# Handing one phase of a two-phase kernel over to the next: where a scaling, two splits and a table load stand in ScalarE's and VectorE's order

## The chip, the cores and the metric

The kernel runs on one core of a Trainium2 chip. The metric is the device time of one execution in microseconds, median of several runs. Engines are named as in the profile: PE (TensorE, matrix products), PEld (its weight loads, which run beside the products), DVE (VectorE), ACT (ScalarE), POOL (GpSimd) and SP (SyncE, which issues nearly all DMAs). Each engine takes its instructions in the order in which the program lists them, and waits on semaphores for what other engines must have done.

## What is computed

An attention block without softmax, with a normed output, feeds a feed-forward block with the activation g = h * erf(softplus(h)). All of it is in float32.

```python
kv = np.einsum('bhsd,bhse->bhde', k, v)        # (8, 8, 576, 64) each
out = np.einsum('bhsd,bhde->bhse', q, kv)
rms = np.sqrt(np.mean(out * out, axis=-1, keepdims=True) + 1e-06)
x = (out / rms * g_norm)                       # then to (4608, 512)
h = x @ w_in                                   # (512, 2048)
sp = np.maximum(h, 0.0) + np.log1p(np.exp(-np.abs(h)))
g = h * erf(sp)
result = g @ w_out                             # (2048, 512)
```

## The kernel before

The 4608 tokens are worked off in nine tiles T of 512 tokens: 0 to 7 hold the first 512 tokens of each batch entry, tile 8 the 64 left over of all eight. The hidden width of 2048 is cut into 16 blocks of 128; one block of one tile is called a unit and is numbered n = 16 T + f. Four units make a batch.

A float32 product can be made of cheaper products in a reduced format (FP32R). For this each operand is *split* into three forms (lines 533 to 551): `upper` on ScalarE scales x by 1 + 2^-13 and stores it rounded ("high"); `lower` on VectorE makes "low" = x - high (L538) and "both" = 4096 low + high (L541). A product of split operands is then two sums in PSUM: n_ps, of the forms high and low (two products for each block of 128), and m_ps, of "both" (one product for each). The result is n_ps times 4095 plus m_ps, up to a scale that the weights carry: ScalarE scales n_ps into SBUF (`AF.Copy` with `scale=SHIFT - 1.0`), and VectorE's `add` (L575) adds m_ps.

There are two phases. In the first one, tiles 0 and 1, the weights stay in SBUF; the loop at `for n in range(FIRST * FC + 1)` goes through units 0 to 31, with the attention of the next tile in pieces between them (`steps`). Tile 0 uses plain float32 products, tile 1 mostly split ones. On the way the weights are split and written to DRAM. In the second phase, tiles 2 to 8, split weights are read back from DRAM for every batch, and each batch consists of four `hidden` products (h of four units) and four `result` products.

The hand-over between the phases is what the change concerns. It covers units 24 to 31. `whole` is 28, `BATCH` 4.

- Units 24 to 27 are *held*: their gated values (g = h * erf(softplus(h)), made by `gates` as one VectorE product of h and s, L904) aren't multiplied by the output weights within the loop. `hold` splits them into `g_held` while units 29 to 31 are worked on: unit 24 at n = 29, units 25 and 26 at n = 30, unit 27 at n = 31. `held_sums` then multiplies them by split weights that stayed in SBUF (`w_place`).
- For each unit n of tile 1 the loop issues: PE's `hidden` (n_ps, m_ps); the scaling of n_ps into h (ACT, L1030); the addition of m_ps (DVE, L575); gates of earlier units; splits of weights while there are any; Softplus (ACT, L1050); attention pieces; `hold`. From unit 28 on h goes to a tile `old_h`, which becomes the first batch of the second phase. The two banks with the tag `h` hold n_ps and m_ps of each unit in turn, so n_ps of a unit needs the scaling of the unit before to be done, and its m_ps the addition.
- `held_sums` runs when the loop is over. It lets the last attention piece of tile 2 do its `mean` (two products with mean_w, the table of log and exp, then Ln, Exp and Square on ScalarE, L476 to L478). On PE it issues the products of "both" of the held units into the four banks o_ps (which already hold the sums of units 16 to 23), and the n_ps sums of output groups j = 0 and 1, in the order units 24 and 25, unit 26, unit 27. Then `norm` (three VectorE steps, L484, L487, L496, and a transposition) gives x of the last quarter of tile 2, and `split` splits it into `x_forms`. A loop over j = 0 to 3 issues the n_ps sums of groups 2 and 3 (their banks are those of groups 0 and 1, so they wait for the scalings of these), the Erf of units 28 to 31 in twos, the scaling of n_ps[j] into e (L954), and the addition of o_ps[j] (L575).
- The gates of units 28 to 31 follow at the end of the loop. Then the pools of the first phase are closed, and pools of the second (w_out_p, for output weights) take their room; the first loads of output weights (`load_parts("out", BATCH)`, L845 on SP) wait until the last user of that room is done. w_in tiles of the first batch are loaded earlier, at n = 29 to 31.
- ScalarE's functions live in tables: one set for Ln and Exp (L113), one for Softplus (L116), one with Erf (loaded ahead of the first Erf that needs it, L960). Each change of set is a table load of its own.

The order of PE's, ScalarE's, VectorE's and SP's instructions is that of the program text (a manual schedule).

Of the kernel before, what the change touches and what calls it, by code (L numbers as in the profile page):

```python
# [50 lines left out]
BATCH = 4  # L51
# [18 lines left out]
def kernel(  # L70
# [462 lines left out]
    def upper(x, high):  # L533

        nc.scalar.activation(high, x, AF.Copy, scale=1.0 + 2.0**-13)  # L535
# [18 lines left out]
    def thirds(x, high, low, both):  # L554
        upper(x, high)
        lower(x, high, low, both)
# [346 lines left out]
    def gates(n):  # L903
        nc.vector.tensor_tensor(out=hs[n], in0=hs[n], in1=ss[n], op=ALU.mult)  # L904

    g_held = {}

    def hold(n):

        i = 2 * (n - whole + BATCH)  # L910
        tiles = [pair_tile("out", i + k, FP32R, "g_held") for k in range(2)]
        forms = g_held[n] = tiles[0][:, 0], tiles[0][:, 1], tiles[1][:, 0]
        thirds(hs[n], *forms)

    def held(ps, n, j, forms, start, stop):
        for form in forms:
            nc.tensor.matmul(  # L917
                ps,
                lhsT=g_held[n][form][:, j * P : j * P + P],
                rhs=w_held[n % FC][form],  # L920
                start=start and form == forms[0],
                stop=stop and form == forms[-1],
            )
# [5 lines left out]
    def held_sums():  # L929

        mean, norm, split = ending
        mean()
        units = range(whole - BATCH, whole)
        n_ps = [None] * J
        all_e = wide.tile([P, J, DM], FP32, name="e", tag="a")
        es.update((j, all_e[:, j]) for j in range(J))
        for j in range(2):
            n_ps[j] = ps_h.tile([P, G], FP32, name="n_ps", tag="h")
        for group in (units[:2], units[2:3], units[3:]):
            for n in group:  # L940
                both_held(n)
            for j in range(2):
                for n in group:
                    held(n_ps[j], n, j, (0, 1), n == units[0], n == units[-1])
        norm()
        split()
        for j in range(J):
            if j >= 2:
                n_ps[j] = ps_h.tile([P, G], FP32, name="n_ps", tag="h")
                for n in units:  # L950
                    held(n_ps[j], n, j, (0, 1), n == units[0], n == units[-1])
            if j >= 2:
                erf(range(whole + 2 * j - 4, whole + 2 * j - 2))
            nc.scalar.activation(es[j], n_ps[j], AF.Copy, scale=SHIFT - 1.0)  # L954
            add(es[j], o_ps[j])
        softplus_table()

    def erf(units):
        for i in units:
            nc.scalar.activation(ss[i], ss[i], AF.Erf)  # L960

    for n in range(FIRST * FC + 1):
        T, f = divmod(n, FC)
        if n == FC:
            early_room.close()
            late = ctx.enter_context(tc.tile_pool(name="late", bufs=1))
            x_new = ctx.enter_context(tc.tile_pool(name="x_new", bufs=1))
            acc = ctx.enter_context(tc.tile_pool(name="acc", bufs=1))
            w_in_p = ctx.enter_context(tc.tile_pool(name="w_in_p", bufs=BATCH))
            low = low_room.enter_context(tc.tile_pool(name="low", bufs=1))  # L970
            forms = late.tile([P, 3, KC, G], FP32R, name="x_forms0")
            x_forms[FIRST] = [forms[:, i] for i in range(3)]
        if T < FIRST:
            if f == 0:
                steps = pieces_of(T + 1)

            if due(0 if n == 2 * (BATCH - 1) else 1):
                weights()
            while kept:
                keep_prepared()  # L980
            for piece in steps[f][3]:
                piece()
            for key in list(w_new)[:2]:
                w_lower(*key)
            for piece in steps[f][0]:
                piece()
        while due(0):
            weights()
        done = n - LAG + 1
        if T == 0 and done >= 0:  # L990
            gates(done)
        if T == FIRST - 1:
            if f == 0:
                x_high = wide.tile([P, KC, G], FP32R, name="x_high", tag="a")
                x_low = low.tile([P, KC, G], FP32R, name="x_low")
                for i in range(0, KC, 2):
                    upper(xT[T][:, i : i + 2], x_high[:, i : i + 2])
                for i in range(0, KC, 2):
                    lower_only(xT[T][:, i : i + 2], x_high[:, i : i + 2], x_low[:, i : i + 2])
        if T == FIRST - 1 and f >= WHOLE:  # L1000
            n_ps, m_ps = hidden(T, f, turns=False)
        elif T < FIRST:

            if n >= AHEAD:
                plain[n] = ps_h.tile([P, G], FP32, name="h_ps", tag="h")
                blocks = [(n, c) for c in range(KC)]
            elif n == 0:
                for i, (pool, tag) in enumerate(((ps_now[0], "at"), (ps_now[0], "at"), (ps_o, "o0"))):
                    plain[i] = pool.tile([P, G], FP32, name="h_ps", tag=tag)
                blocks = [(i, c) for c in range(2) for i in range(2)]  # L1010
                blocks += [(2, 0), (2, 1)] + [(i, 2) for i in range(3)] + [(0, KC - 1)]
            else:
                blocks = [(n, KC - 1)]
            for i, c in blocks:
                nc.tensor.matmul(  # L1015
                    plain[i],
                    lhsT=blocks_of(one(w_in_sb, i % FC))[:, c],
                    rhs=xT[T][:, c, :],
                    start=(c == 0),
                    stop=(c == KC - 1),  # L1020
                )
        if T < FIRST:
            if n == whole:
                old_h = acc.tile([P, BATCH, G], FP32, name="h", tag="e")
            h = hs[n] = old_h[:, n - whole] if n >= whole else unit("h_sb")
            s = ss[n] = unit("s_sb")
            if n in plain:
                nc.scalar.copy(h, plain.pop(n))
            else:
                nc.scalar.activation(h, n_ps, AF.Copy, scale=SHIFT - 1.0)  # L1030
                add(h, m_ps)
            if T == FIRST - 1:
                if f == 1:
                    x_both = wide.tile([P, KC, G], FP32R, name="x_both", tag="b")
                    for i in range(0, KC, 2):
                        both_only(x_high[:, i : i + 2], x_low[:, i : i + 2], x_both[:, i : i + 2])
                    x_forms[T] = x_high, x_low, x_both
                if done < whole - 2:
                    gates(done)
                for key in list(w_new):  # L1040
                    w_lower(*key)
                for key in to_cut[f]:
                    w_upper(*key)
                if n == whole + 1:
                    gates(whole - 2)
                    gates(whole - 1)
            if T == FIRST - 1 and f and f % BATCH == 0:
                erf(range(n - BATCH // 2, n))
                softplus_table()
            nc.scalar.activation(s, h, AF.Softplus)  # L1050
            for piece in steps[f][1]:
                piece()
            for i in {whole + 1: (0,), whole + 2: (1, 2), whole + 3: (3,)}.get(n, ()):
                hold(whole - BATCH + i)
            if f % BATCH == BATCH - 1 and n < whole:
                apart = T == FIRST - 1 and f < FC - 1
                erf(range(n - BATCH + 1, n + 1 - (BATCH // 2 if apart else 0)))
                if not apart:
                    softplus_table()
            if T == FIRST - 1:  # L1060
                load_parts("in", {FC - 3: 2, FC - 2: 1, FC - 1: 1}.get(f, 0))
        if LAG <= n < whole - BATCH + LAG:
            T2, f2 = divmod(n - LAG, FC)
            last = n - LAG == FC - 1
            project(f2, hs[n - LAG], last)
            if last:
                sums(acc, "e")
                for j in range(J):
                    store(T2, j, es.pop(j))
        if n == FIRST * FC:  # L1070
            held_sums()
        if T < FIRST:
            for piece in steps[f][2]:
                piece()
            fetch_some(4)
    for n in range(whole, FIRST * FC):
        gates(n)


# [187 lines left out]
```

## Time and profile before

| what | us |
|---|---|
| median of 3 runs | 910.99 (910.78 to 911.67) |
| the profiled execution, whole | 910.55 |
| its span (first to last instruction) | 908.8 |
| products of the second phase, from the first hidden product to the end | from 241.34 |
| PE busy, DVE busy, ACT busy in the span | 897.4, 765.1, 594.7 |

The span is what the trace covers; the execution around it takes 1.75 us more. A row of the timeline gives start, length, engine, line, operation, output and input tiles, number of instructions, and in brackets how long the engine had been idle before it and what it waited for. Consecutive instructions of a kind overlap a little in the records: products of 128x512 start 0.228 us apart and last 0.39 us each; ACT functions of 128x512 start 0.52 us apart and last 0.58 to 0.63; DVE steps of that size start 0.60 us apart, or 0.72 if one needs the one before, and last 0.69.

### The profile page before, as it was taken

To read this page: it belongs to the slowest core of one execution; us is meant where nothing else is said; L and a number is where in the kernel's file an instruction comes from. 1 tells how busy PE (TensorE), PEld (TensorE's weight loads), DVE (VectorE), ACT (ScalarE), POOL (GpSimd) and SP (SyncE) were. 2 spreads that over 40 slices of the span, in tenths; PEclk is the share of its full clock that TensorE was granted. 3 is DMA by queue.
4 is the path that set the end of the run, shared out by engine and by line. 5 is a ranking of instruction groups with operands and counts; after the bars stand their busy time and mean duration, and the time that the engine had idled before them with its cause. 6 is when DMAs were issued, how large, how long until landed. Compare 5 with 4: busy or idle time off the path is not lost.

```text
span 908.8 us, 13463 instructions
## 1 busy us (share of the span) xinstructions
PE 897.4 (99%) x4954; PEld 673.0 (74%) x4954; DVE 765.1 (84%) x1103; ACT 594.7 (65%) x789; POOL 4.7 (1%) x14
## 2 busy tenths in 40 slices
PE   8999999999899999999999999999999999999998
PEld 4444446666688888888888888888888888888886
DVE  5899959998688888888888888888898888887777
ACT  5976667776766667666666666666666766665552
POOL 2000000000000000000000000000000000000000
PEclk9999999999999999999999999999999999999999
DMA  9967308999399988999899879988797778778871
GB/s 283 296 221 232 101 24 292 363 348 359 121 383 376 354 298 268 368 316 316 274 326 370 302 254 318 366 300 304 282 351 261 270 302 311 290 286 314 324 265 50
DMA packets 137505, 259.89 MB, mean 286 GB/s; under 512 B 78880, under 2 KB 87328, under 8 KB 137440
## 3 DMA queue, kind: packets, MB, share of 16 engines
q1 hardware_dynamic: 136704, 258.09, 80.7%
q10 hardware_dynamic: 544, 0.82, 0.3%
q8 instruction: 39, 0.64, 0.3%
q14 instruction: 26, 0.21, 0.1%
q0 software_dynamic: 192, 0.13, 0.1%
HBM read 224.40 MB, written 34.60 MB: 285 GB/s over the span
## 4 chain that ended last, share of the span: by engine, by line
PE 92%; DVE 3%; DMA 2%; ACT 2%; SPq 0%; issue 0%; DVEq 0%
PE n_ps L600 48%; PE m_ps L600 24%; PE o_ps L656 9%; PE h_ps L1015 6%; PE at_ps L426 2%; PE at_ps L412 2%; DMA w_out_parts<-w_out 1%; DMA q_sb<-in_q_dram 1%; PE at_ps L465 1%; PE at_ps L464 1%; PE n_ps L917 1%; DMA w_raw<-in_moe_w_out_dram 1%; DVE w_in_sb L282 0%; DVE h L904 0%; DVE w_e L277 0%
## 5 line engine op out<-in xcount | busy, mean ns | idle before, releaser
L600 PE MATMUL n_ps<-w_out_parts,g_forms 128*128 128x512 f32 (+1 forms) x936 | 231.1, 389 | 0.1
L600 PE MATMUL n_ps<-x_forms,w_in_parts 128*128 128x512 f32 x896 | 224.0, 392 | 0.0
L600 PEld LDWEIGHTS n_ps<-w_out_parts,g_forms 128*128 128x128 f32 x936 | 173.8, 188 | 35.6 <-DMA w_out_parts<-w_out 0.6
L600 PEld LDWEIGHTS n_ps<-x_forms,w_in_parts 128*128 128x128 f32 x896 | 166.8, 188 | 35.1
L575 DVE TENSOR_TENSOR h<-m_ps,h 128x512 f32<-128x512 f32 x116 | 78.1, 687 | 59.3 <-PE m_ps L600 57.2
L600 PE MATMUL m_ps<-w_out_parts,g_forms 128*128 128x512 f32 x464 | 124.1, 390 | 0.0
L600 PE MATMUL m_ps<-x_forms,w_in_parts 128*128 128x512 f32 x448 | 119.8, 390 | 0.0
L1173 ACT ACTIVATE h<-n_ps 128x512 f32<-128x512 f32 x112 | 66.1, 593 | 74.6 <-PE n_ps L600 74.4
L1178 ACT ACTIVATE s<-h 128x512 f32<-128x512 f32 x112 | 68.4, 629 | 70.7 <-DVE h L575 70.6
L600 PEld LDWEIGHTS m_ps<-w_out_parts,g_forms 128*128 128x128 f32 x464 | 87.2, 188 | 18.5
L600 PEld LDWEIGHTS m_ps<-x_forms,w_in_parts 128*128 128x128 f32 x448 | 84.2, 188 | 17.4
L575 DVE TENSOR_TENSOR e<-m_ps,e 128x512 f32<-128x512 f32 x116 | 80.1, 692 | 15.2 <-PE m_ps L600 5.3
L656 PE MATMUL o_ps<-w_out_sb,h_sb 128*128 128x512 f32 x192 | 87.0, 596 | 0.0
L541 DVE SCALAR_TENSOR_TENSOR g_forms<-g_forms 128x1024 fp32r<-128x1024 f32 x58 | 71.1, 1225 | 2.0
L538 DVE TENSOR_TENSOR g_forms<-h,g_forms 128x1024 fp32r<-128x1024 f32 x58 | 70.6, 1217 | 1.2 <-ACT g_forms L535 1.1
L535 ACT ACTIVATE g_forms<-h 128x1024 fp32r<-128x1024 f32 x58 | 58.4, 1049 | 16.9 <-PE m_ps L600 11.1
L570 DVE SCALAR_TENSOR_TENSOR e<-n_ps,e 128x512 f32<-128x512 f32 (+1 forms) x89 | 60.4, 678 | 7.3 <-PE n_ps L600 7.3
L1015 PE MATMUL h_ps<-xT,w_in_sb 128*128 128x512 f32 x144 | 65.1, 596 | 1.2 <-DVE w_in_sb L282 1.1
L1227 DVE TENSOR_TENSOR h<-h,s 128x1024 f32<-128x1024 f32 x56 | 65.9, 1217 | 0.0
L656 PEld LDWEIGHTS o_ps<-w_out_sb,h_sb 128*128 128x128 f32 x192 | 35.6, 190 | 38.2 <-issue 37.3
L116 ACT ACT_TABLE_LOAD x43 | 55.2, 1283 | 0.8
L1015 PEld LDWEIGHTS h_ps<-xT,w_in_sb 128*128 128x128 f32 x144 | 27.0, 190 | 35.3 <-issue 31.3
(147 smaller groups left out, 1033.9 us busy)
## 6 DMA issues: line engine op xcount, KB each, us to landing
w_out_parts<-w_out SPq DMA_DIRECT2D x116, 768.0 KB, 6.9
w_in_parts<-w_in SPq DMA_DIRECT2D x112, 768.0 KB, 6.7
w_in<-w_new SPq DMA_DIRECT2D x16, 768.0 KB, 4.5
k_sb<-in_k_dram SPq DMA_DIRECT2D x32, 288.0 KB, 5.7
v_sb<-in_v_dram SPq DMA_DIRECT2D x31, 288.0 KB, 5.9
w_raw<-in_moe_w_in_dram SPq DMA_DIRECT2D x16, 512.0 KB, 5.8
w_raw<-in_moe_w_out_dram SPq DMA_DIRECT2D x8, 1024.0 KB, 5.3
out_dram<-e SPq DMA_DIRECT2D x32, 256.0 KB, 3.6
```

The source lines that it names most:

```text
L116: nc.scalar.preload_act_table_set("softplus")
L535: nc.scalar.activation(high, x, AF.Copy, scale=1.0 + 2.0**-13)
L538: nc.vector.tensor_tensor(out=low, in0=x, in1=high.bitcast(FP32), op=ALU.subtract)
L541: nc.vector.scalar_tensor_tensor(out=both, in0=low.bitcast(FP32), scalar=SHIFT, in1=high.bitcast(FP32), op0=ALU.mult, op1=ALU.add,)
L570: nc.vector.scalar_tensor_tensor(out=out_, in0=ps, scalar=scale, in1=out_, op0=ALU.mult, op1=ALU.add)
L575: nc.vector.tensor_tensor(out=out_, in0=ps, in1=out_, op=ALU.add)
L600: nc.tensor.matmul(ps[:, cols], lhsT=weights(form, k), rhs=moving(form, k)[:, cols], start=(form == forms[0] and k == 0), stop=(form == fo ...
L656: nc.tensor.matmul(o_ps[j], lhsT=g[:, j * P : j * P + P], rhs=one(w_out_sb, f), start=(f == 0), stop=last,)
L1015: nc.tensor.matmul(plain[i], lhsT=blocks_of(one(w_in_sb, i % FC))[:, c], rhs=xT[T][:, c, :], start=(c == 0), stop=(c == KC - 1),)
L1173: nc.scalar.activation(h[:, i], n_ps, AF.Copy, scale=SHIFT - 1.0)
L1178: nc.scalar.activation(s[:, i], h[:, i], AF.Softplus)
L1227: nc.vector.tensor_tensor(out=part(h, half), in0=part(h, half), in1=part(s, half), op=ALU.mult)
```

## The change

It reorders what ScalarE and VectorE do from unit 29 to the end of `held_sums`.

- `hold` is parted into `hold_upper` (ScalarE) and `hold_lower` (VectorE). The upper parts of units 24 and 25 come at n = 29, of 26 and 27 at n = 30; the lower parts of 24 and 25 at n = 30, of 26 and 27 at n = 31, each behind the addition to h of that n.
- Three gates in one place (units 25, 26 and 27 at n = 29) become two (25, 26) there and one (27) at n = 30, behind the addition to h.
- In `held_sums`, the set with Erf is named right behind `norm`; the scaling of group 0 is issued ahead of `split`, that of group 1 behind it. The n_ps sums of groups 2 and 3, additions of groups 0 and 1, Erf and gates of units 28 and 29, scaling of group 2, Erf of 30, scaling of group 3, Erf of 31, and the additions of groups 2 and 3 follow in that order. The gates of units 30 and 31 remain behind `held_sums`.

```diff
-    def hold(n):
+    def hold_upper(n):
...
-        forms = g_held[n] = tiles[0][:, 0], tiles[0][:, 1], tiles[1][:, 0]
-        thirds(hs[n], *forms)
+        g_held[n] = tiles[0][:, 0], tiles[0][:, 1], tiles[1][:, 0]
+        upper(hs[n], g_held[n][0])
+
+    def hold_lower(n):
+        lower(hs[n], *g_held[n])
...
         norm()
+
+        def scaled(j):
+            nc.scalar.activation(es[j], n_ps[j], AF.Copy, scale=SHIFT - 1.0)
+
+        nc.scalar.preload_act_table_set("sigmoid_and_others")
+        scaled(0)
         split()
-        for j in range(J):
-            if j >= 2:
-                n_ps[j] = ps_h.tile([P, G], FP32, name="n_ps", tag="h")
-                for n in units:
-                    held(n_ps[j], n, j, (0, 1), n == units[0], n == units[-1])
-            if j >= 2:
-                erf(range(whole + 2 * j - 4, whole + 2 * j - 2))
-            nc.scalar.activation(es[j], n_ps[j], AF.Copy, scale=SHIFT - 1.0)
+        scaled(1)
+        for j in range(2, J):
+            n_ps[j] = ps_h.tile([P, G], FP32, name="n_ps", tag="h")
+            for n in units:
+                held(n_ps[j], n, j, (0, 1), n == units[0], n == units[-1])
+        for j in range(2):
+            add(es[j], o_ps[j])
+        erf((whole, whole + 1))
+        for n in (whole, whole + 1):
+            gates(n)
+        scaled(2)
+        erf((whole + 2,))
+        scaled(3)
+        erf((whole + 3,))
+        for j in range(2, J):
             add(es[j], o_ps[j])
         softplus_table()
...
-                if done < whole - 2:
-                    gates(done)
+                if n <= whole + 2:
+                    gates(done + max(0, n - whole - 1))
...
                 if n == whole + 1:
                     gates(whole - 2)
-                    gates(whole - 1)
...
-            for i in {whole + 1: (0,), whole + 2: (1, 2), whole + 3: (3,)}.get(n, ()):
-                hold(whole - BATCH + i)
+            for i in range(*{whole + 1: (0, 2), whole + 2: (2, 4)}.get(n, (0,))):
+                hold_upper(whole - BATCH + i)
+            for i in range(*{whole + 2: (0, 2), whole + 3: (2, 4)}.get(n, (0,))):
+                hold_lower(whole - BATCH + i)
...
-    for n in range(whole, FIRST * FC):
+    for n in range(whole + 2, FIRST * FC):
         gates(n)
```

## The prediction

> **What bounds the kernel now.** I read the page's busy table first, then the chain of waits. TensorE is busy for 99% of the span, so a gain can only come from the little that is left.
>
> ```profile
> span 908.8 us, 13463 instructions
> PE 897.4 (99%) x4954; PEld 673.0 (74%) x4954; DVE 765.1 (84%) x1103; ACT 594.7 (65%) x789; POOL 4.7 (1%) x14
> ```
>
> A table of stretches gives PE 642.87 us busy out of 643 us from 262 us to 905 us. Nothing waits there, so whatever the middle of the kernel gains or loses reaches the end unchanged. The middle is 217 to 256 us, where the first phase hands over to the second. The chain of waits, asked for 205 to 262 us, leaves PE at 217.1 us and comes back only for one stretch:
>
> ```profile
> 223.05 0.69 DVE h L575
> ...
> 228.97 0.52 ACT g_held L535
> 229.49 0.02 issue
> 229.50 1.28 ACT L113
> ...
> 232.19 0.64 ACT u L478
> ...
> 234.30 0.76 DVE x L496
> ...
> 235.09 0.63 ACT x_forms L535
> 235.72 0.49 ACT e L954
> 236.21 0.04 issue
> 236.25 5.26 PE n_ps L917 x16
> ```
>
> Columns: start, length, what. Softplus of the last unit and the split of unit 27 hold ScalarE until 229.5 us. Then come the root's table, three functions, three VectorE steps of the norm, the split's scaling of x (L535), and only then the scaling of the first sums (L954), which empties the bank that PE waits for. PE's timeline shows both halts:
>
> ```profile
> 223.79 1.20 PE L600 MATMUL m_ps<-x_both,w_new 128*128 128x512 f32 x4 [0.63 <-DVE h L575]
> 236.25 5.25 PE L917 MATMUL n_ps<-w_place,g_held 128*128 128x512 f32 x16 [3.04 <-ACT e L954]
> ```
>
> The brackets hold idle time and releaser. The second row also takes 5.25 us for 16 products. The table of stretches says why (PE, PEld, DVE, ACT, POOL busy, then PEclk):
>
> ```profile
> 235.00:237.00 2.00, 0.74 (x2) 0.65 (x3) 1.93 (x4) 1.89 (x4) 0.00 (x0) 0.67 0.00 0
> 237.00:239.00 2.00, 2.00 (x7) 1.52 (x6) 1.37 (x3) 1.99 (x3) 0.00 (x0) 0.50 0.00 0
> 239.00:241.00 2.00, 2.00 (x10) 1.66 (x9) 0.67 (x1) 1.45 (x4) 0.00 (x0) 0.97 0.00 0
> ```
>
> The granted clock is half until about 239 us. Last, the waits of the weight loads and of SP's queue between 195 and 262 us:
>
> ```profile
> PEld n_ps L600 <- DMA w_out_parts<-w_out: 0.6, 1, 0.6
> SPq L845 <- DVE h L904: 15.9, 1, 15.9
> ```
>
> The second phase's first output weights are requested only after the last gate product (L904, ending at 245.26 us). They land at 255.39 us and hold PE once more.
>
> **What the skill says.** TensorE: Matmul & The Clock Gate, section "Part 1: The HAM clock gate", has PE fall to half its clock after an idle window of some 3.4 us and return after as long busy. This trace roughly agrees: 3.04 us idle, then half clock for some 3 us; after 0.63 us idle the clock stayed 1.00. The same page, "Architectural detail", calls ScalarE and VectorE strict FIFO; here the scaling at 235.62 us stood behind L535 though its sums were complete at about 232.8 us. ScalarE: Activation LUTs, "What ACT_TABLE_LOAD costs", gives 1283 ns plus 1380 ns of drain. The load itself is 1.28 us here too, but the next function starts 0.02 us later, so I take 1.28. The same page, "Table sets", lists erf in the sigmoid set and cheap functions in every set, so the copies under the early table need no other load; that copies need none is seen here (scalings run under the log table at 235.62 us).
>
> **The change part by part.** The built programs show PE's and SP's orders unchanged, and no instruction added or dropped. ScalarE and VectorE are reordered from 217 us on. I carry the old starts forward: VectorE starts 0.60 us apart (0.72 when dependent), ScalarE 0.52, PE 0.228 per product.
>
> *Splits in twos.* After gates of units 25 and 26 (217.80, 218.40), the four steps of unit 24's split and the third gate no longer stand ahead of the attention step. That step waits for its square (219.03) and runs 219.05 to 221.2. The addition to h of unit 30 then waits only for its product (221.32): 221.41 to 222.10, formerly 223.05. So m_ps of unit 31 starts right behind its n_ps at 222.99, not 223.79: 0.80 saved. Late next: gate 27 at 222.01, then splits of 24 and 25, the last ending at 225.35 (formerly 226.37). PE wants it at 225.30, so the old stall of 0.47 at L917 shrinks to about 0.1, and PE is now 1.02 ahead. h of unit 31 is added at 225.26 to 225.95; the 0.24 stall of the second bank goes, making about 1.2. Splits 26 and 27 end at 227.27 and 228.60, ahead of their products (228.2 and 230.0). PE ends its first sums at about 232.0, formerly 233.2.
>
> On ScalarE, g_held 26 and 27 (ready 223.7) and the copy of h (223.68 to 224.28) precede softplus of unit 31 at 225.97. With no g_held behind it, the root's table starts at 226.61, formerly 229.50: 2.89 earlier. The three functions end at 229.94 and x is normed at 234.30 - 2.89 + 0.76 = 232.17.
>
> *Erf's table sooner.* The load runs 229.95 to 231.23, while PE is on its first sums and VectorE on the norm: cost nothing. It used to stand at 236.71, behind the scalings.
>
> *Scaling ahead of the split.* The first sum's last two products started at 232.14 before and were complete at about 232.14 + 2 x 0.228 + 0.16 (a product's record lasts 0.39) = 232.76; now 232.76 - 1.2 = 231.56. Its scaling runs 231.60 to 232.20 with nothing in front, and PE starts its third sum at 232.24, formerly 236.25: 4.01 saved (1.2 of it is the part above). PE's gap is some 0.3 us, so I expect no half clock: 16 products take 16 x 0.228 = 3.65 instead of 241.34 - 236.25 = 5.09, saving 1.44. The split of x goes at 232.2, the second scaling at 232.72 to 233.3, in time for the fourth sum at 234.06; the remaining steps of the split end at 234.3. PE enters the second phase at about 235.9, formerly 241.34. **Together 5.45 us.**
>
> *Additions, Erf and gates interleaved.* VectorE: additions at 234.2 and 234.8, gates 28 and 29 at 235.4 and 236.0, additions at 236.6 and 237.2 (third and fourth scalings end at 234.9 and 236.7), gates 30 and 31 at 237.8 and 238.4, ending at 239.09. Formerly 245.26: 6.17 earlier. The last Erf ends at 237.2, so the last gate waits for none. SP's request moves by as much, with the DMA queues just as empty (0.00 busy before it in both). Landing at 255.39 - 6.17 = 249.22 meets PE wanting the fourth tile at 254.87 - 5.45 = 249.42. The stall of 0.56 goes: **5.45 + 0.56 = 6.0 us.** What queues behind the request on SP (k, v, w_in) moves with it. The fourth w_in tile, requested at 228.02 for a use now at 245.6, has 17 us; the longest landing there is 10.8. Each hidden product's banks come free ahead of use (the tightest: fourth scaling ending at 236.7, bank wanted at 237.7).
>
> *What is unknown.* Whether the half clock really goes: between 0 and 1.44 saved; I take 1.44 since 0.63 idle cost nothing. Whether the weights land in time: between a stall of 0.56 + 0.8 (if they land a microsecond slower) and none; I take none, as they meet an empty queue in both. The added waits on ScalarE: at worst the norm is late and holds the second scaling behind x's split; its slack is 0.76, and another microsecond would cost 0.3. On the other side PE's remaining gaps (0.3 + 0.1) bound any further gain at 0.4.
>
> The profiled execution took 910.55 us around its span of 908.8; its span becomes 902.8 and the execution 904.55. It stands 0.44 below the median of 910.99, which gives 910.99 - 6.0 = **905.0**.
>
> **The rivals.**
> - *Half clock stays* (8%): the short gap falls into an unlucky window. For: the window's phase isn't seen. Against: 0.63 us idle at 1.00. 4.01 + 0.56 stay: 911.0 - 4.6 = 906.4.
> - *Additions not freed* (6%): unit 30's addition is still late, through the square or the attention step. PE keeps its 0.63 halt and ScalarE's chain slips alike: 0.8 less, 905.8.
> - *Weights are the real bound* (3%): the output weights land near the old 255.4, because something besides the gate holds their request, and PE merely waits longer there. For: they did hold PE. Against: SP's 15.9 us wait ends at the gate. 911.0, no change.
> - *Slower* (5%): the new phase between PE and DMA makes the 0.56 stall on w_out recur at each of the 28 batches' first output products. DMA is busy for 0.67 to 1.05 of its time after 262 us. At 0.56 each it costs 15.7 against 6.0 gained: 920.7. It decides from 6.0 / 28 = 0.21 us per batch. Against: the gate moves 6.17 and PE 6.0, so the phase hardly changes, and it never recurred before.
> - The forecast itself: 78%.
>
> **How the numbers follow.** About 0.2% (1.8 us) is what a measurement of this kernel can tell from no change. Forecast and the first two rivals lie beyond that: faster 0.92. The third gives same 0.03, the fourth slower 0.05. The forecast's own 0.4 below, its unknowns of up to about 1.4 above, the first two rivals and the medians' scatter (0.9 in three runs) make 903.8 to 907.4.
>
> **What would show it.** PE's m_ps of unit 31 without the L575 wait; the third and fourth of the held units' n_ps sums starting near 232.2 after under 0.5 us idle, 3.7 us long at clock 1.00; the first second-phase product near 236; the last gate ending near 239; no weight-load wait on w_out_parts. I am wrong if PE still idles over 1 us between 231 and 236, if the clock dips, or if any PE wait appears after 250 us.

## The result and the profile after

| | before | after |
|---|---|---|
| median, 6 runs each | 911.19 (909.11 to 911.67) | 904.27 (904.04 to 904.75) |
| the profiled execution, whole / span | 910.55 / 908.8 | 904.33 / 902.5 |

The ratio is 0.9927, with a 95% interval of 0.9915 to 0.9940: 5.5 to 7.7 us faster. The forecast was 905.0.

The first two lines of the page show how little PE's total says: its busy time falls by 2.5 us only, while the span falls by 6.3. The rest of the gain is idle time that is gone.

```profile
span 902.5 us, 13462 instructions
PE 894.9 (99%) x4954; PEld 671.3 (74%) x4954; DVE 765.2 (85%) x1103; ACT 594.7 (66%) x789; POOL 4.7 (1%) x14
```

The chain of waits for 205 to 262 us, which before left PE for 19 us at 217.1, stays on PE now and leaves it once, for two thirds of a microsecond (start, length, what):

```profile
230.68 0.47 PE n_ps L920 x2
231.15 0.02 issue
231.17 0.61 ACT e L951
231.78 0.04 issue
231.82 3.94 PE n_ps L920 x16
235.76 1.84 PE n_ps L600 x8
```

L951 is the scaling that was L954, L920 the held units' products that were L917. The scaling starts 0.02 us after the first sum is complete. PE's timeline (start, length, line, tiles, idle before and its releaser) has the gap, the 16 products, the first hidden product and the first result product:

```profile
231.82 3.94 PE L920 MATMUL n_ps<-w_place,g_held 128*128 128x512 f32 x16 [0.24 <-ACT e L951]
235.59 2.01 PE L600 MATMUL n_ps<-x_forms,w_in_parts 128*128 128x512 f32 x8
...
248.03 1.98 PE L600 MATMUL n_ps<-w_out_parts,g_forms 128*128 128x512 f32 x8
```

The eight products of that last row took 0.42 us longer before, with a wait for the output weights inside:

```profile
253.78 2.40 PE L600 MATMUL n_ps<-w_out_parts,g_forms 128*128 128x512 f32 x8
```

The table of stretches (PE, PEld, DVE, ACT, POOL busy, PEclk, DMA share, GB/s) has full clock in every stretch from 230 to 900 us; before, it stood at 0.50 for one such stretch and at 0.67 for the one ahead of it:

```profile
231.00:233.00 2.00, 1.76 (x8) 1.17 (x7) 1.97 (x3) 1.83 (x4) 0.00 (x0) 1.00 0.46 126
233.00:235.00 2.00, 2.00 (x11) 1.62 (x10) 1.97 (x5) 1.93 (x4) 0.00 (x0) 1.00 0.00 0
```

ScalarE's timeline shows the new order: root's table, Erf's table, first scaling, x's split, second scaling.

```profile
226.17 1.28 ACT L113 ACT_TABLE_LOAD   x1
...
229.50 1.28 ACT L953 ACT_TABLE_LOAD   x1
231.17 0.60 ACT L951 ACTIVATE e<-n_ps 128x512 f32<-128x512 f32 x1 [0.39 <-PE n_ps L920]
231.75 0.63 ACT L535 ACTIVATE x_forms<-x 128x512 fp32r<-128x512 f32 x1
232.29 0.58 ACT L951 ACTIVATE e<-n_ps 128x512 f32<-128x512 f32 x1
```

And SP waits 9.8 us for the last gate where it waited 15.9. The output weights are requested at 238.69 us; before, it was 245.41 (SP's timeline, of before first, then of after):

```profile
SPq L845 <- DVE h L904: 9.8, 1, 9.8
```

```profile
245.41 2.03 SPq L845 DMA_DIRECT2D w_out_parts<-w_out  x4
```

```profile
238.69 2.16 SPq L845 DMA_DIRECT2D w_out_parts<-w_out  x4
```

Two traces don't start alike: PE reaches the attention product ahead of unit 30 (L412), the last mark in front of everything the change touches, at 217.01 us before and at 216.52 after. That 0.49 us belongs to the start of the kernel. To keep it out, the traces are compared from that product on, at two places: B, the first hidden product of the second phase, and C, the first product of the second result group. From C to the end of the span every trace takes 651.3 or 651.4 us, so what a kernel gains up to C it keeps.

| run | median us | L412 | B - L412 | C - L412 | C against before |
|---|---|---|---|---|---|
| before | 911.19 | 217.01 | 24.33 | 40.41 | |
| after | 904.27 | 216.52 | 19.07 | 34.70 | -5.71 |
| e1 pairs only | 906.72 | 216.89 | 20.17 | 36.79 | -3.62 |
| e2 sums only | 906.76 | 216.54 | 21.52 | 37.16 | -3.25 |
| e3 table late | 904.87 | 217.02 | 19.34 | 35.07 | -5.34 |
| e4 split first | 905.80 | 216.62 | 20.15 | 35.78 | -4.63 |
| e5 gap filled | 909.11 | 215.78 | 23.03 | 39.63 | -0.78 |
| e6 gap part filled | 910.41 | 216.55 | 24.61 | 40.77 | +0.36 |
| e7 gates last | 905.10 | 216.97 | 19.08 | 35.22 | -5.19 |
| e8 after again | 904.47 | 216.70 | 19.09 | 34.71 | -5.70 |
| e9 sum first | 904.26 | 216.43 | 18.70 | 34.37 | -6.04 |
| e10 gates first | 904.36 | 216.86 | 18.69 | 34.39 | -6.02 |

e6 has one time, the others are medians. The median of the kernel before differed between the batches of runs: 910.55 beside e1 to e4, 910.62 beside e5 to e7, 909.97 beside e8 to e10. Part of the reason is in the last of the experiments.

### The profile page after: what moved, and what is told of

It reads as the page before. It is cut to its first block, busy times and chain, and to the rows that moved or that the text cites. A ratio compares the mean times of both kernels' runs of the same rounds, so it can differ in the third digit from the quotient of the medians.

```text
span 902.5 us, 13462 instructions
## 1 busy us (share of the span) xinstructions
PE 894.9 (99%) x4954; PEld 671.3 (74%) x4954; DVE 765.2 (85%) x1103; ACT 594.7 (66%) x789; POOL 4.7 (1%) x14
## 4 chain that ended last, share of the span: by engine, by line
PE 97%; DVE 1%; ACT 1%; DMA 1%; issue 0%; DVEq 0%; SPq 0%
PE n_ps L600 49%; PE m_ps L600 24%; PE o_ps L656 9%; PE h_ps L1031 6%; PE at_ps L426 2%; PE at_ps L412 2%; PE n_ps L920 1%; PE at_ps L464 1%; PE at_ps L465 1%; PE warm_ps L803 1%; DMA w_raw<-in_moe_w_out_dram 1%; PE o_ps L920 0%; DVE w_e L277 0%; PE o_ps L723 0%; DVE w_in_sb L282 0%; PE ms_ps L730 0%
```

## The experiments

### The two halves of the change alone: e1 and e2

e1 keeps the reordered splits and gates and takes `held_sums` as it was. e2 does the reverse.

```diff
 # e1, against the changed kernel; the gates also go back behind everything
-        nc.scalar.preload_act_table_set("sigmoid_and_others")
-        scaled(0)
         split()
-        scaled(1)
...
+        for j in range(J):
...
+                erf(range(whole + 2 * j - 4, whole + 2 * j - 2))
+            nc.scalar.activation(es[j], n_ps[j], AF.Copy, scale=SHIFT - 1.0)
+            add(es[j], o_ps[j])
```

> The change with only its first part: splits in twos and the third gate behind the addition to h; the sums of the held units as in the kernel before. My theory: the two PE halts of 0.63 and 0.24 go and ScalarE reaches the root's table 2.9 us sooner, so the first sums' scaling ends about 3.3 us sooner even behind x's split; PE's gap shrinks from 3.04 to about 1.3, no half clock, PE enters the second phase some 4.6 us sooner, and the output weights (gates all at the end) hold it again for about 0.8: 906.2 us, 5.0 below the kernel before. Rival (this part is worth only the two halts, and the gain sits in the scaling moved ahead): 910.0 us, PE gap near 3, clock still dips.

> The change with only its second part: Erf's table sooner, the scaling ahead of x's split, Erf, gates and additions interleaved; splits as in the kernel before. My theory: the root's chain is as late as before, so the first scaling ends at about 234.75 and PE starts again 1.45 us sooner than before after a gap of 1.6; no half clock, another 1.4; the weights' stall of 0.56 goes: 907.8 us, 3.4 below before. If the clock still dips, 909.2. Rival (the parts add up to the whole, so with 5.0 of 6.9 in the pairs only 1.9 are left here): 909.3 us with a clock of 1.00.

e1: 906.72 us, ratio 0.9955 (0.9939 to 0.9972). e2: 906.76 us, ratio 0.9957 (0.9942 to 0.9972). PE's timelines, of e1 first, then of e2 (the scaling L951 has another line number in each kernel: L957 in e1, L948 in e2):

```profile
233.28 3.94 PE L920 MATMUL n_ps<-w_place,g_held 128*128 128x512 f32 x16 [1.32 <-ACT e L957]
...
251.73 0.73 PE L600 MATMUL n_ps<-w_out_parts,g_forms 128*128 128x512 f32 x2 [0.72 <-DMA w_out_parts<-w_out]
```

```profile
234.31 3.92 PE L917 MATMUL n_ps<-w_place,g_held 128*128 128x512 f32 x16 [1.57 <-ACT e L948]
```

Gaps of 1.32 and 1.57 us stand where 1.3 and 1.6 were expected, the products take 3.9 us in both, so the clock stays full in both. In e1 the late gates turn part of the gain into a wait for the output weights, as expected, but the whole is less than I expected: 3.62 us at C and 3.8 in the medians of its batch, for 5.0. PE enters the second phase 4.16 us sooner (B, 24.33 - 20.17) where I had put 4.6, and the weights take back 0.54. My 5.0 didn't follow from its own parts, which allow for about 4.4 (4.6 less the 0.24 by which the stall was to grow from 0.56 to 0.8). The rival of e1, which left only the two small halts to the pairs, is out. The additive rival of e2 asked for a rest of 1.9; 3.25 came. The halves overlap: 3.62 + 3.25 = 6.87 against 5.71 for both. Each alone leaves the clock full, and the 1.3 us of the half clock can be won only once; that it is the main part of the overlap is argued, not tried by itself.

In e2 ScalarE's timeline shows what becomes late next if the chain to the root isn't sooner: the table load itself.

```profile
232.36 1.28 ACT L950 ACT_TABLE_LOAD   x1
233.66 0.60 ACT L948 ACTIVATE e<-n_ps 128x512 f32<-128x512 f32 x1
```

The scaling follows the load after 0.02 us, and the first sum had been complete for more than a microsecond (its last two products started at 231.67). Only with the pairs does the early load lie in PE's shadow.

### The early table and the early scaling, each taken out: e3 and e4

```diff
 # e3
-        nc.scalar.preload_act_table_set("sigmoid_and_others")
 # e4
-        scaled(0)
         split()
+        scaled(0)
```

> The changed kernel without the early naming of Erf's table, which then stands ahead of the first Erf, behind the second scaling. My theory: it delays the third scaling from 233.97 to about 235.2, which still frees its bank within 0.3 us of PE wanting it, and the last gate by 0.2 us: 904.5 us, within 0.3 of the changed kernel's 904.3. Rival (the load on the path costs its whole length): 905.6 us, 1.28 above, all of it a PE wait before the first hidden product.

> The changed kernel with x's split ahead of the first scaling again, all else as changed. My theory: the scaling starts at about 232.3 instead of 231.17, PE's gap grows from 0.24 to about 1.3, the clock stays 1.00, and the weights' request slips by less than PE: 905.4 us, 1.1 above the changed kernel's 904.3. Rival (this order is the main part, some 4 us, half clock included): 908 us or more, clock dipping to 0.50.

e3: 904.87 us, ratio 0.9937 (0.9922 to 0.9952). At C it is 0.37 later than the changed kernel, a little more than the 0.3 I allowed and far from the rival's 1.28. The load now stands behind the second scaling, and the third, which frees the bank of the first hidden product, comes late (ScalarE's timeline, then the waits of the weight loads):

```profile
233.38 1.28 ACT L975 ACT_TABLE_LOAD   x1
234.67 1.15 ACT L975 ACTIVATE s_sb<-s_sb 128x512 f32<-128x512 f32 x2
235.73 0.58 ACT L951 ACTIVATE e<-n_ps 128x512 f32<-128x512 f32 x1
```

```profile
PEld n_ps L600 <- ACT e L951: 0.5, 1, 0.5
```

e4: 905.80 us, ratio 0.9947 (0.9932 to 0.9962), at C 1.08 later than the changed kernel; 1.1 was expected. PE's gap is 1.31, the clock full:

```profile
233.01 3.92 PE L920 MATMUL n_ps<-w_place,g_held 128*128 128x512 f32 x16 [1.31 <-ACT e L951]
```

So within the whole change, by one trace each, the early scaling is worth 1.1 us and the early table 0.4.

### The half clock by itself: e5 and e6

```diff
 # e5: range(3); e6: range(1), the kernel before otherwise
-            held(o_ps[j], n, j, (2,), False, n == whole - 1)
+            held(o_ps[j], n, j, (2,), False, stop)
...
+        for again in range(3):
+            both_held(whole - 1, again == 2)
         norm()
         split()
```

> The kernel before with PE's idle stretch filled: the four products of 'both' of unit 27 are issued three times more behind the first sums (the output then has that term four times), nothing else moves. My theory: the gap shrinks from 3.04 to about 0.3, the clock stays 1.00 and the 16 products take 3.9 instead of 5.25, so PE enters the second phase 1.3 sooner; but the output weights are requested as late as before, so their stall grows from 0.45 to about 1.8 and the time stays at that of the kernel before, within 0.3 us. Rival (the half clock is a loss of its own, on the path): 1.3 below before. Second rival (the half clock isn't due to idling): 5.25 us for the 16 products again.

> The kernel before with the same four products issued once more (that term is in the output twice), which leaves a gap of about 2.1 us. Gaps of 1.3 and 1.6 us left the clock at 1.00 in the runs so far, one of 3.04 halved it. My theory: 2.1 is still short enough, clock 1.00, 16 products in 3.9. Rival: any gap over 2 halves it, about 5.2.

e5, 909.11 us, ratio 0.9988 (0.9981 to 0.9995). PE's timeline:

```profile
231.83 2.88 PE L917 MATMUL o_ps<-w_place,g_held 128*128 128x512 f32 x12
235.03 3.94 PE L917 MATMUL n_ps<-w_place,g_held 128*128 128x512 f32 x16 [0.32 <-ACT e L956]
...
253.44 0.73 PE L600 MATMUL n_ps<-w_out_parts,g_forms 128*128 128x512 f32 x2 [0.68 <-DMA w_out_parts<-w_out]
```

Twelve products that change nothing in the order of any other engine give the clock back: the 16 products take 3.94 instead of 5.25, and B is 1.30 sooner. The times say the same: each of the 20 runs of e5 lists a mean granted clock of 0.999 or 1.000, while 15 of the 23 runs of the kernel before in that batch list 0.995 to 0.998. So the idle stretch brings the half clock about; it doesn't do so in every execution, as the other eight of the 23 show (below, two groups of times). My theory erred about the rest. I had the weights' request fixed; it went out at 243.21 - 215.78 = 27.43 us behind L412, in the kernel before at 245.41 - 217.01 = 28.40, because the third and fourth scaling, and with them Erf, the additions and the gates, wait for those 16 products. So 0.78 of the 1.30 arrive at C, and the weights take the other 0.52. The ratio of the times gives 1.1 us, with an interval of 0.5 to 1.7. So neither my theory (no change, within 0.3 us) nor the first rival (1.3 us) came out; the truth lies between.

e6 leaves a gap of 2.17 us, and the clock dips all the same, but later (table of stretches):

```profile
235.00:237.00 2.00, 1.20 (x5) 1.02 (x6) 1.97 (x4) 1.98 (x4) 0.00 (x0) 1.00 0.00 0
237.00:239.00 2.00, 2.00 (x7) 1.53 (x7) 0.91 (x2) 1.99 (x4) 0.00 (x0) 0.57 0.00 0
239.00:241.00 2.00, 2.00 (x7) 1.57 (x6) 0.69 (x1) 1.21 (x3) 0.00 (x0) 0.57 0.00 0
```

PE started again at 235.80 and ran at full clock for more than a microsecond before it was halved; the 16 products took 5.53. My theory, that 2.1 us is short enough, is wrong. e6 has one run; in e1, e2 and e4, with gaps of 1.31 to 1.57 us, all 12 runs list 0.999 or 1.000. So 2.17 us can be enough, and with 1.57 us or less it was never seen.

### The weights' request: e7

```diff
-        for n in (whole, whole + 1):
-            gates(n)
...
-    for n in range(whole + 2, FIRST * FC):
+    for n in range(whole, FIRST * FC):
         gates(n)
```

> The changed kernel with the gates of units 28 and 29 back behind all additions, with those of 30 and 31; Erf and scalings as changed. My theory: VectorE then waits for the fourth scaling with work left, the last gate ends about 0.9 later (239.5 instead of 238.6 on the changed kernel's clock), PE's entry into the second phase doesn't move, and as the fourth tile of output weights landed only 0.1 to 0.2 before PE wanted it, PE waits about 0.7 for it: 905.0 us against 904.3. Rival (the request had slack): 904.3 and no wait on the output weights.

905.10 us, ratio 0.9938 (0.9922 to 0.9955). VectorE's timeline shows the empty place that the two gates had filled, PE's the wait:

```profile
236.88 0.69 DVE L575 TENSOR_TENSOR e<-o_ps,e 128x512 f32<-128x512 f32 x1 [0.81 <-ACT e L951]
237.49 2.49 DVE L904 TENSOR_TENSOR h<-h,s_sb 128x512 f32<-128x512 f32 x4
```

```profile
250.25 0.73 PE L600 MATMUL n_ps<-w_out_parts,g_forms 128*128 128x512 f32 x2 [0.24 <-DMA w_out_parts<-w_out]
```

The request is 240.04 - 216.97 = 23.07 us behind L412, in the changed kernel 22.17: 0.90 later. B doesn't move, C is 0.52 later. So the weights had about 0.4 us to spare in the changed kernel (0.90 - 0.52, if the transfers took as long in both), where I had put 0.1 to 0.2, and gates between the additions are worth half a microsecond.

### Further along the same path: e8, e9, e10

e9 moves the gate of unit 27 behind the splits of 24 and 25, and the n_ps products of unit 27 ahead of its products of "both". e10 puts the last gates ahead of the last additions as well. e8 is the changed kernel beside them.

```diff
 # e9 and e10
-        for group in (units[:2], units[2:3], units[3:]):
+        for group in (units[:2], units[2:3]):
...
+        for j in range(2):
+            held(n_ps[j], units[-1], j, (0, 1), False, True)
+        both_held(units[-1])
...
-                if n <= whole + 2:
-                    gates(done + max(0, n - whole - 1))
+                if n <= whole + 1:
+                    gates(done)
...
+            if n == whole + 3:
+                hold_upper(whole - 1)
...
+            if n == whole + 2:
+                gates(whole - 1)
 # e10
-        erf((whole + 2,))
+        erf((whole + 2, whole + 3))
         scaled(3)
-        erf((whole + 3,))
+        for n in (whole + 2, whole + 3):
+            gates(n)
```

> The changed kernel as it is, beside the two that follow: 904.3 us, 0.9927 of the kernel before, within 0.4 us.

> The changed kernel with the third gate (unit 27) behind the splits of units 24 and 25, unit 27's scaled form behind the copy of h, and the n_ps products of unit 27 ahead of its products of 'both'. My theory: the stall of 0.37 on the split of unit 25 and PE's gap of 0.24 in front of the third sum both go nearly, so PE enters the second phase 0.4 sooner; the weights' request hangs on VectorE's unbroken row of steps behind x and doesn't move, but had some 0.4 to spare: 903.9 us, with a wait on the output weights just about to appear. Rival (the table load of Erf's set now ends last, so nothing is gained): 904.3 us.

> As the one before, and with the last Erf ahead of the fourth scaling and the gates of units 30 and 31 ahead of the third and fourth additions. My theory: the last gate ends 1.2 sooner, the request goes out as much sooner, PE's entry is as in the one before, so no wait on output weights even with the gain: 903.9 us, or 0.1 less than the one before if that one met a wait. Rival (late scaling or additions hold the banks of the first hidden products): slower than the changed kernel, with a PE wait between 235 and 243.

e8: 904.47 us, ratio 0.9937 (0.9924 to 0.9950); its trace repeats the first one's to 0.02 us. e9: 904.26 us, ratio 0.9937 (0.9924 to 0.9950). e10: 904.36 us, ratio 0.9940 (0.9926 to 0.9953). The times of the three can't be told apart. The 903.9 that I expected of e9 and e10 was not reached. The trace of e9 shows what was wanted: hardly any idle time in front of the 16 products (0.09 us from the end of the record ahead, in the changed kernel 0.23), B 0.37 and C 0.33 sooner than there. The scaling now stands straight behind the table load, which ends last, as the rival had it.

```profile
231.35 3.94 PE L920 MATMUL n_ps<-w_place,g_held 128*128 128x512 f32 x16
```

```profile
229.41 1.28 ACT L956 ACT_TABLE_LOAD   x1
230.70 0.60 ACT L954 ACTIVATE e<-n_ps 128x512 f32<-128x512 f32 x1
```

In e10 the request goes out 1.19 us sooner (237.84 - 216.86 = 20.98 against 22.17), and yet a short wait appears:

```profile
PEld n_ps L600 <- DMA w_out_parts<-w_out: 0.2, 1, 0.2
```

In its table of stretches the queues moved 215 GB/s in the microsecond from 241 us and 276 in the next; in the changed kernel's they ran at 399 and 430 in these two. So an earlier request isn't by itself an earlier landing. Why the transfers were slower there wasn't tried. The rival of e10 is out: B is as in e9 (18.69 and 18.70).

### Two groups of times before: e11 and e12

> The kernel before as it is, one more look. Its times over the runs so far fall in two groups, 908.4 to 909.5 and 910.3 to 911.9, with little between; those of the changed kernel and of the one with PE's gap filled don't. My theory: the two groups are executions in which the clock dips in PE's gap of 3.04 us or doesn't, so a profiled execution near 908.9 has 16 products in about 3.9 at a clock of 1.00, and one near 911 has them in about 5.2 with the clock at 0.50. Rival (the groups come from the start of the kernel, whose length varies by 1.2 us between traces): the 16 products take about 5.2 in either group.

> The same once more, as one look may fall in the same group as the first trace: near 908.9 us with the 16 products in about 3.9 at a clock of 1.00, or near 911 with about 5.2; the rival has about 5.2 in both groups.

Both executions fell into the upper group (910.74 and 910.78 us) and repeat the first trace: 5.42 and 5.37 us for the 16 products.

```profile
236.26 5.42 PE L917 MATMUL n_ps<-w_place,g_held 128*128 128x512 f32 x16 [3.08 <-ACT e L954]
```

No run of the lower group left a trace. But every run lists its mean granted clock, and this sorts the 40 runs of the kernel before that stand beside e1 to e10 without one exception:

| group | runs | us | mean granted clock |
|---|---|---|---|
| lower | 14 | 908.42 to 909.47, median 909.0 | 0.999 to 1.000 |
| upper | 26 | 909.82 to 911.89, median 910.8 | 0.995 to 0.998 |

All 12 listed runs of the changed kernel have 0.999 or 1.000. An estimate from the traces of before fits: some 3.4 us at half clock lose 1.7 us of clock in 909, which makes a mean of 0.998. So my theory of the two groups is borne out by the clock: in 14 of 40 executions the clock did not fall, though the kernel is the same. That it was the gap's dip which was missing is inferred, since 235 to 241 us is where all three traces of before have their only dip ahead of the end of PE's work. The clock isn't all of it. The groups' medians lie about 1.9 us apart, while the filled gap of e5 brought 0.78 at C; the start of the kernel, which the rival names, may add to it (L412 came at 217.01 to 217.05 us in the three traces of before and at 215.78 in that of e5). And eight runs between 911.4 and 911.9 us, at 0.995 or 0.996, lost about twice the clock of one such stretch by the same estimate; where, no trace shows.

This bears on what the change is worth. In the batch of e8 the changed kernel (904.47) gains 6.3 us on the five runs of the upper group (median 910.73) and 4.6 on the five of the lower (909.09); the medians of all give 5.5 there and 6.9 in the first comparison. The traces agree: 5.71 us behind L412 against an execution with the half clock, and, as an estimate, 5.71 - 0.78 = 4.9 against one without.

## Why the prediction was right

Times here count from L412, since the forecast was built on the trace before. In the main the steps came as forecast and in the forecast sizes.

- *Addition to h behind no split.* Forecast 4.40 us behind L412, measured 4.41 (220.93 - 216.52). The product m_ps of unit 31 starts 0.78 sooner; forecast 0.80. Right.
- *What is late next.* The split of unit 25 ends at 8.36, forecast 8.34. The wait for it is 0.37 on the weight load instead of the 0.1 forecast: the load of the weights comes 0.24 us sooner than the place of the product that I took. PE's lead there was right all the same, 1.00 for 1.02, because PE waits for that split in both kernels. The working had a lead of 0.80 and a stall shorter by 0.37, which would be more; the traces have 0.90 and 0.10.
- *Root's table.* 2.84 us sooner; forecast 2.89. PE's last first sum starts 1.13 sooner; forecast 1.2.
- *Scaling ahead of the split.* The third sum starts 3.94 sooner (15.30 against 19.24); forecast 4.01. The credit is shared: e4 gives 1.1 of it to the order of scaling and split, and the pairs alone (e1) bring 2.85 (16.39 against 19.24).
- *Erf's table at no cost.* It ended at 230.78, and the first sum was complete 0.37 later. Right, with that little to spare; e2 shows it on the path when PE's sums aren't longer than the root's chain.
- *Half clock gone.* Forecast 1.44, measured 1.32: the products with the start of the next sum take 3.77 and not 16 x 0.228 = 3.65. By e5 the cause is the idle stretch, and by itself this term would bring 0.78 at C, not 1.3: the rest arrives only because the weights' request moves too. The bound of that term was the doubtful one, and e6 shows why: a gap of 2.2 us wouldn't have been short enough. The 0.24 us that came were. The term also took for certain what happens in some executions only: in 14 of 40 the kernel before kept its clock.
- *Entry into the second phase.* 5.26 sooner, forecast 5.45: the sum of the terms above.
- *Last gate.* 6.14 sooner; forecast 6.17.
- *Weights' stall gone.* It is gone, and worth 0.45, not 0.56. I had read the wait of the weight load; the products lose less, since the loads run ahead of them. e7 shows that it went with the gates between the additions, and that 0.4 us are to spare.

The sum behind L412 is 5.26 + 0.45 = 5.71 for the 6.0 forecast; the terms mis-sized are the clock by 0.12, the stall by 0.11 and the third sum by 0.07. The span fell by 6.3 because the trace after also started 0.49 us sooner. How near 904.27 came to the forecast 905.0 was in part luck. The median rests on more than the 5.71 of the traces: it fell by 6.9, because five of the six runs of before belong to the upper group by their times, two of them near its top (911.61 and 911.67). The base of the forecast, 910.99 from three runs, lay in that group too. With before at 909.97, as in the batch of e8, the same change of the kernel is worth 5.5. Of the rivals, full clock was kept (1.00 in every stretch), the additions were freed, the weights weren't the bound, and PE shows no wait in the later batches: in the trace after, the longest that its weight loads wait behind 255 us is 0.4, at L412, as before.

## What to carry to other kernels

When one engine is busy for 99% of the span, list its few idle stretches and follow each back through every engine's queue: here a bank that PE needed was freed by a function whose input had been complete for about 2.8 us and which stood behind one that wasn't ready. Count a stretch of idle PE with what it can do to the clock, and look at the clock of many runs before taking one trace's dip for the rule (26 of 40 runs show it here). Count moved work also by the request that hangs on it: 0.45 us of the gain lay in a DMA whose trigger was the last of four gates. Parts that remove the same loss don't add up (6.87 for two halves, 5.71 together), so try each alone and the whole without each.

## What the runs showed of the hardware that was not expected

The same gap of PE halves the clock in some executions and not in others. With 3.04 to 3.08 us it did in all three traces of the kernel before, yet 14 of 40 runs of that kernel list a mean clock of 0.999 or more. With 2.17 us (e6, one run) it did; with 1.31 to 1.57 us (e1, e2, e4) it did in none of 12 runs.

The half clock lasted equally long wherever it was traced, about 3.4 us: (0.33 + 0.50 + 0.03) x 2 / 0.5 from the stretches of before, (0.43 + 0.43) x 2 / 0.5 from those of e6, and the same for e11 and e12. What differed was where it began. Worked out from the same stretches, that was about 235.7 us before, 2.5 us into the gap and 0.6 ahead of PE's restart at 236.25; in e6 it was about 237.3, 1.5 us behind the restart at 235.80, so that PE worked through the whole of it. That is why the shorter gap cost no less: the 16 products took 5.53 us in e6 and 5.25 before, against 3.9 at full clock. What sets the beginning isn't shown here.
